# GpSimd's second sum of two pairs made to wait for Vector's two, in the last part of a gated mix of a state-space convolution and a spectral filter

## The chip, the cores and the metric

One core of one Trainium2 chip. The metric is the device time of one execution in microseconds; the median of three runs stands for a kernel. Lower is better. All data are float32.

## The reference

The input u is a sequence of 2048 positions by 640 channels. Two results are made of it and mixed by a gate that depends on the position:

```python
    g = _sigmoid((x * gate_w).sum(-1, keepdims=True))
    a = _A_ref(...)   # y = irfft(rfft(u, 4096) * rfft(K, 4096))[:2048] + u * D_skip, K made of exponentials of the position
    b = _B_ref(...)   # irfft2(rfft2(x) * (w_r + 1j * w_i))
    return g * a + (1 - g) * b
```

Branch a is a long convolution along the sequence, one kernel K per channel, done with transforms of length 4096. Branch b is a filter on the two-dimensional spectrum. Only branch a, in its last part, is touched by the change.

## The kernel before, in words

The transforms are written as matrix products. A transform of length 4096 has two stages: 64 values at a time (`stage1`, L335), then 64 at a time with the twiddle factors folded into the tables (`stage2`, L348). The 640 channels are worked through in four quarters of 160 (index c). A quarter's spectrum is a set of 33 small blocks, two to a column; 17 columns (16 full ones of 128 partitions, and one half, of 64) make a quarter. A column's 128 partitions hold two blocks of 64 (j = 0 and 1).

Earlier parts make the spectrum of u (kept in DRAM as `u_d`), the kernels K (`k_d`), and branch b up to its last stage (`s3e_d`). The last part, `phase_d`, starts at about 438 us of the profile. For each quarter it takes groups of four columns (`groups`; the half column is a group by itself), and for each group:

- `fronts`: per *pair* of columns, `stage2` makes the spectrum of K in PSUM (`p_s`, L348, one of three double banks). Vector multiplies it with the spectrum of u (`us`, loaded from `u_d`) in two products: `ma` (L795: real by real, imaginary by imaginary) and `mb` (L796: crosswise). One input of each lies in PSUM, the other in SBUF. Then come four sums, which make the complex product `t2` out of them: for each block j the difference of the two halves of `ma` (L800, the real part, into partitions 0 to 63 of `t2`), and the sum of the two halves of `mb` (L801, the imaginary part, into partitions 64 to 127). Both inputs of a sum lie in SBUF. Vector takes the real part of j = 0 and the imaginary part of j = 1, and GpSimd the other two, so a full pair costs each engine one L800 and one L801, each 64 partitions by 320 elements.
- `backs`: one or two groups later (the list `late`), the first stage of the inverse transform (L814, `p_i`, reading `t2`), a copy by ScalarE into `s3` (L816, for the half column L818), and the DMA of that to `s3_d` on ScalarE's queue (L823, for the half column L820).

Beside these run, at rates that `merge` sets, `stage1` of the next quarter (L335, with ScalarE's copy L336), and the last stage of branch b and of branch a: `last_e` (TensorE `p_e` at L160, Vector's gated product `oe` at L876) and `last_c` (TensorE `p_c` at L893, Vector's gated product `ot` at L898, and the add of both on GpSimd, L899, with the DMA of the result, L901). The three kinds of `p_s`, and `p_i`, share three PSUM buffers; `p_e` and `p_c` share two. After the last group, `s3_d`'s last rows are written (L820, L823) and read again (L866), and the last products (L893, L896) and output DMAs (L904) end the kernel.

Each engine works its instructions in the order in which they stand in its queue. That order comes from the tile layer, which sorts what the streams issue by when it estimates it to be ready; a semaphore wait is put in wherever an instruction depends on another engine's.

## Time and profile before

| | |
|---|---|
| median of three runs | 607.03 us (604.68 to 610.24) |
| the profiled execution | 608.74 us, span of its instructions 607.0 us |
| granted TensorE clock, mean | 0.966 (1.00 from 438 to 578 us) |
| busy over the span: PE / DVE / ACT / POOL | 535.8 / 500.2 / 364.8 / 267.0 us |
| busy from 438 to 578 us: PE / DVE / ACT / POOL | 128.18 / 118.81 / 40.17 / 73.59 us of 140 |

PE is TensorE (PEld its weight loads), DVE is Vector, ACT is ScalarE, POOL is GpSimd, SP is the engine that only issues DMAs. A line of a group reads: line, engine, operation, out<-in, shape, count | busy us, mean ns of one | idle time of that engine just before, and what ended it. A line of the timeline reads: start and duration in us, engine, line, operation, count, and in brackets how long the engine had been idle and who released it. [...] ACTq and SPq are the queues in which an engine issues DMAs; a piece named DMA in the chain of waits is the transfer itself.

### The profile page before, as it was taken

To read this page: it belongs to the slowest core of one execution; us is meant where nothing else is said; L and a number is where in the kernel's file an instruction comes from. 1 tells how busy PE (TensorE), PEld (TensorE's weight loads), DVE (VectorE), ACT (ScalarE), POOL (GpSimd) and SP (SyncE) were. 2 spreads that over 40 slices of the span, in tenths; PEclk is the share of its full clock that TensorE was granted. 3 is DMA by queue.
4 is the path that set the end of the run, shared out by engine and by line. 5 is a ranking of instruction groups with operands and counts; after the bars stand their busy time and mean duration, and the time that the engine had idled before them with its cause. 6 is when DMAs were issued, how large, how long until landed. Compare 5 with 4: busy or idle time off the path is not lost.

```text
span 607.0 us, 16654 instructions
## 1 busy us (share of the span) xinstructions
PE 535.8 (88%) x7084; PEld 405.6 (67%) x7084; DVE 500.2 (82%) x748; ACT 364.8 (60%) x659; POOL 267.0 (44%) x246
## 2 busy tenths in 40 slices
PE   9688979989968989989798999898989999999874
PEld 7576657766656657676566676565878877787631
DVE  5971597598899989999999899979399796987974
ACT  4556775576846876888589888799723332231210
POOL 4931252053525344454326335416254347547441
PEclk9899989989989996998899999999999999999998
DMA  8787204245612320332250233006685989889776
GB/s 341 293 288 268 79 5 151 69 154 181 239 43 67 97 87 13 108 118 109 67 151 12 75 97 110 24 28 200 224 346 184 356 273 299 291 271 310 225 231 239
DMA packets 48083, 101.98 MB, mean 168 GB/s; under 512 B 3316, under 2 KB 32776, under 8 KB 46248
## 3 DMA queue, kind: packets, MB, share of 16 engines
q1 hardware_dynamic: 24888, 67.74, 32.3%
q10 hardware_dynamic: 20080, 22.52, 11.9%
q0 software_dynamic: 3040, 10.65, 5.3%
q8 instruction: 56, 0.92, 0.6%
q14 instruction: 19, 0.16, 0.1%
HBM read 60.91 MB, written 39.98 MB: 166 GB/s over the span
## 4 chain that ended last, share of the span: by engine, by line
PE 51%; DVE 27%; ACT 9%; DMA 8%; issue 4%; POOL 1%; ACTq 0%; DVEq 0%; POOLq 0%; SPq 0%
PE p_eo L551 8%; PE p_s L348 8%; PE p_s L335 6%; PE p_e L638 5%; PE p_k L693 4%; PE p_i L814 4%; PE p_p L649 3%; DVE q L652 3%; PE p_d L518 2%; DVE t L801 2%; PE p_i L565 2%; PE p_t L502 2%; DVE ma L795 2%; PE p_c L893 2%; PE p_d L519 2%
## 5 line engine op out<-in xcount | busy, mean ns | idle before, releaser
L679 POOL TENSOR_TENSOR y<-e,sc 128x512 f32<-128x512 f32 x40 | 56.7, 1418 | 131.0 <-ACT sc L665 60.3
L348 PE MATMUL p_s<-t,w 128*64 128x160 f32 x1056 | 92.4, 314 | 10.2 <-ACT ut L382 5.1
L348 PEld LDWEIGHTS p_s<-t,w 128*64 128x64 f32 x1056 | 76.5, 139 | 21.4 <-ACT ut L382 6.0
L640 ACT ACTIVATE e<-p_e 128x512 f32<-128x512 f32 x120 | 68.6, 602 | 22.7 <-PE p_e L638 20.4
L551 PE MATMUL p_eo<-td,pmt 107*128 107x321 f32 x204 | 69.0, 459 | 3.9 <-ACT pmt L505 3.9
L693 PE MATMUL p_k<-x,y 128*32 128x64 f32 x2560 | 63.6, 229 | 9.8 <-DVE x L677 2.9
L693 PEld LDWEIGHTS p_k<-x,y 128*32 128x32 f32 x2560 | 46.1, 113 | 38.0 <-issue 29.4
L652 DVE SCALAR_TENSOR_TENSOR q<-q,p_p 128x512 f32<-128x512 f32 x80 | 53.4, 681 | 13.5 <-ACT q L651 11.8
L336 ACT COPY t<-p_s 128x512 f32<-128x512 f32 x40 | 24.6, 623 | 65.2 <-PE p_s L335 41.8
L638 PE MATMUL p_e<-rm,par 128*128 128x512 f32 x120 | 58.7, 519 | 3.4 <-ACT e L640 2.8
L680 POOL TENSOR_TENSOR y<-e,sc 128x512 f32<-128x512 f32 x40 | 54.5, 1362 | 6.5 <-ACT sc L666 6.5
L800 POOL TENSOR_TENSOR t<-ma 64x320 f32<-64x320 f32 x32 | 28.0, 875 | 61.4 <-DVE ma L795 51.8
L551 PEld LDWEIGHTS p_eo<-td,pmt 107*128 107x128 f32 x204 | 38.4, 198 | 19.6 <-ACT pmt L505 6.9
L677 DVE TENSOR_TENSOR x<-e,cx 128x1024 f32<-128x1024 f32 x40 | 48.6, 1214 | 2.2 <-ACT cx L668 2.2
L651 ACT ACTIVATE q<-p_p 128x512 f32<-128x512 f32 x80 | 46.5, 592 | 4.2 <-PE p_p L649 3.8
L649 PE MATMUL p_p<-rp,par 128*128 128x512 f32 x80 | 43.5, 548 | 4.5 <-DVE q L652 4.5
L814 PE MATMUL p_i<-t,w 128*64 128x160 f32 x528 | 42.7, 300 | 4.4 <-POOL t L801 3.4
L335 PE MATMUL p_s<-c,kt 128*64 128x128 f32 x640 | 43.0, 274 | 3.9 <-DVE mb L796 2.0
L335 PEld LDWEIGHTS p_s<-c,kt 128*64 128x64 f32 x640 | 38.0, 136 | 12.6 <-issue 7.7
L816 ACT COPY s<-p_i 128x640 f32<-128x640 f32 x32 | 21.8, 694 | 40.0 <-PE p_i L814 30.4
L335 PE MATMUL p_s<-c,u 128*64 128x128 f32 x640 | 41.5, 278 | 2.5 <-ACT ut L382 2.5
L795 DVE TENSOR_TENSOR ma<-p_s,us 128x640 f32<-128x640 f32 (+1 forms) x36 | 28.2, 784 | 18.8 <-PE p_s L348 11.5
(153 smaller groups left out, 1181.5 us busy)
## 6 DMA issues: line engine op xcount, KB each, us to landing
u_d<-ut SPq DMA_DIRECT2D x32, 320.0 KB, 2.6
us<-u_d ACTq DMA_DIRECT2D x16, 640.0 KB, 6.0
s_d<-s ACTq DMA_DIRECT2D x15, 640.0 KB, 8.3
t<-s_d SPq DMA_DIRECT2D x14, 640.0 KB, 5.9
ww<-in_w_l SPq DMA_DIRECT2D x8, 642.0 KB, 4.0
ue<-u_d SPq DMA_DIRECT2D x8, 640.0 KB, 4.4
k_d<-kt SPq DMA_DIRECT2D x4, 1280.0 KB, 7.6
kt<-k_d SPq DMA_DIRECT2D x8, 640.0 KB, 5.9
```

Source lines behind the costliest of these rows:

```text
L335: nc.tensor.matmul(p[64 * ri:64 * ri + 64, j, :], src(i + j), e1[ri], start=True, stop=True)
L348: ins = nc.tensor.matmul(p[64 * j:64 * j + 64, i, 160 * ri:160 * ri + 160], w2[:, x, 64 * ri:64 * ri + 64], t1[:, x // 2 if x < 32 else K0 ...
L551: P.matmul(p[:, :E], st.pmt[:DC, c, w, j, :], tv[:DC, w, c, :], start=c == 0, stop=c == 2)
L638: P.matmul(p[:, :], pars[t], rm[:, c:c + 512], start=True, stop=True)
L640: st.exp = S.activation(ef[:, c:c + 512], p[:, :], AF.Exp)
L649: P.matmul(p[:, :], pars[t], rp[:, c:c + 512], start=True, stop=True)
L652: V.scalar_tensor_tensor(out=qf[:, c:c + 512], in0=qf[:, c:c + 512], scalar=MAGIC, in1=p[:, :], op0=ALU.subtract, op1=ALU.subtract)
L677: V.tensor_tensor(out=x[:, 0].rearrange("p d (h j) -> p d h j", h=2), in0=e[:, :, 0:64].rearrange("p d (h j) -> p d h j", h=2), in1=cx.uns ...
L679: G.tensor_tensor(out=y[:, 1], in0=e[:, :, 64:96], in1=sc[:, 0], op=ALU.mult)
L680: G.tensor_tensor(out=y[:, 0], in0=e[:, :, 64:96], in1=sc[:, 1], op=ALU.mult)
L693: P.matmul(st.pb[32 * r:32 * r + 32, o, :], y[:, ri, 4 * qq + JR[r], :], x[:, ri, 4 * qq + JR[r], :], start=t % 2 + qq + 1 - ri == 0, stop ...
L814: T.mm = P.matmul(p[x:x + 64, i // 2, 160 * (i % 2):160 * (i % 2) + 160], T.w3[:, k0 + h + i, x:x + 64], t2[:, h + i, :], start=True, stop ...
```

## The change

The four sums of a pair are written by a helper `part(eng, j, im)`, and the last line makes GpSimd's imaginary part (j = 0) depend on Vector's last sum of the same pair: on its L801 for a full pair, on its L800 for a half column. Which engine computes which part stays as it is, and so do the shapes. Since the half column has only j = 0, GpSimd has one sum there, and it waits too.

```diff
@@ -794,11 +795,20 @@
             V.tensor_tensor(out=mb[:nl, :hn], in0=pv, in1=uu[:, :, ::-1, :], op=ALU.mult)
-            for j in range(nj):
+            def part(eng, j, im):
                 l = slice(64 * j, 64 * j + 64)
                 o = slice(nj * h + j, nj * (h + hn), nj)
-                (G if j else V).tensor_tensor(out=t2[0:64, o, :], in0=ma[l, :hn, 0, :], in1=ma[l, :hn, 1, :], op=ALU.subtract)
-                (V if j else G).tensor_tensor(out=t2[64:128, o, :], in0=mb[l, :hn, 0, :], in1=mb[l, :hn, 1, :], op=ALU.add)
+                m = mb if im else ma
+                return eng.tensor_tensor(out=t2[64 * im:64 * im + 64, o, :], in0=m[l, :hn, 0, :], in1=m[l, :hn, 1, :], op=ALU.add if im else ALU.subtract)
+            if nj > 1:
+                part(G, 1, 0)
+            last = part(V, 0, 0)
+            if nj > 1:
+                last = part(V, 1, 1)
+            ins = part(G, 0, 1)
+            tc.add_manual_dep(ins.ins, last.ins.name, SYNC, reason="port")
             yield 0.55 * hn
```

`SYNC` is a dependency of the kind that needs a semaphore. In the changed file all four sums have one line, L802; other lines of the last part are 1 lower before the sums and 10 lower behind them than in the changed file (L899 becomes L909, L820 becomes L830).

The queues of TensorE, Vector and SP hold the same instructions in the same order before and after. Two places differ.

On GpSimd's queue, at the end of the second quarter (`t_6306` is the `t2` of its half column, `ot` the add of both branches), before:

```order
L801 TENSOR_TENSOR t_6208<-mb 64x2x160
L801 TENSOR_TENSOR t_6306<-mb 64x160
L899 TENSOR_TENSOR ot<-ot,oe 128x480 x2
L899 TENSOR_TENSOR ot<-ot,oe 128x320
L901 DMA out<-ot 128x1280
```

and now:

```order
L802 TENSOR_TENSOR t_6208<-mb 64x2x160
L909 TENSOR_TENSOR ot<-ot,oe 128x480
L802 TENSOR_TENSOR t_6306<-mb 64x160
L909 TENSOR_TENSOR ot<-ot,oe 128x480
L909 TENSOR_TENSOR ot<-ot,oe 128x320
L911 DMA out<-ot 128x1280
```

One add has moved ahead of the half column's sum.

On ScalarE's queue, at the very end (`s_7085` is the half column of the last quarter, `s_7091` its last group, copied and written in two halves), before:

```order
L823 DMA s_d<-s_7028 128x8x160
L818 COPY s_7085<-p_i_7086 128x160
L816 COPY s_7091<-p_i_7092 128x640
L820 DMA s_d<-s_7085 64x160
L823 DMA s_d<-s_7091 128x4x160
L816 COPY s_7091<-p_i_7103 128x640
```

and now:

```order
L833 DMA s_d<-s_7028 128x8x160
L828 COPY s_7085<-p_i_7086 128x160
L830 DMA s_d<-s_7085 64x160
L826 COPY s_7091<-p_i_7092 128x640
L833 DMA s_d<-s_7091 128x4x160
L826 COPY s_7091<-p_i_7103 128x640
```

The small DMA of the half column has moved ahead of the copy of the last group's first half. That DMA writes a row that the larger DMA ahead of it (`s_7028`) also writes, and waits until that one has landed.

## The prediction

> **What bounds the kernel now.** I read the windows view first, to see which engine has room in the last part (438 to 578 us, the four quarters of columns; what follows is its tail), then the groups by shape, then the timeline of one pair, and last the waits on TensorE. Columns of the windows rows: stretch, its length, busy us (instructions) of PE, PEld, DVE, ACT and POOL, granted clock, DMA share, GB/s.

> ```profile
> 438.00:457.00 19.00, 16.08 (x216) 13.61 (x216) 17.02 (x22) 4.49 (x8) 9.57 (x11) 1.00 0.83 321
> ...
> 489.00:514.00 25.00, 24.05 (x302) 20.02 (x300) 18.68 (x28) 7.67 (x12) 15.17 (x17) 1.00 0.94 302
> ...
> 560.00:578.00 18.00, 15.00 (x170) 11.47 (x168) 17.37 (x26) 4.46 (x7) 8.10 (x10) 1.00 0.73 230
> ```

> Two engines take turns. From 438 to 457 and from 560 to 578 Vector is busy nearly all the time (17.02 of 19, 17.37 of 18) and TensorE is not. From 489 to 514 it is the reverse: TensorE 24.05 of 25 us. A cheaper Vector is worth something only in stretches of the first kind. The groups say what Vector does there:

> ```profile
> L801 DVE TENSOR_TENSOR t<-mb 64x320 f32<-64x320 f32 x30 | 31.5, 1052 | 0.9
> ...
> L800 DVE TENSOR_TENSOR t<-ma 64x320 f32<-64x320 f32 x30 | 19.1, 638 | 0.0
> ```
> ```profile
> L801 POOL TENSOR_TENSOR t<-mb 64x320 f32<-64x320 f32 x30 | 30.2, 1005 | 2.6 <-DVE mb L796 0.4
> L800 POOL TENSOR_TENSOR t<-ma 64x320 f32<-64x320 f32 x30 | 26.3, 876 | 58.3 <-DVE ma L795 48.7 <-issue 9.6
> ```

> The same shape, 64x320, costs Vector 638 ns as its first sum (L800) and 1052 ns as its second (L801). One pair in order of time (start, duration) shows why:

> ```profile
> 446.20 0.82 DVE L795 TENSOR_TENSOR ma<-p_s,us 128x640 f32<-128x640 f32 x1
> 446.94 0.81 DVE L796 TENSOR_TENSOR mb<-p_s,us 128x640 f32<-128x640 f32 x1
> 447.67 0.63 DVE L800 TENSOR_TENSOR t<-ma 64x320 f32<-64x320 f32 x1
> 448.34 1.04 DVE L801 TENSOR_TENSOR t<-mb 64x320 f32<-64x320 f32 x1
> 449.41 0.82 DVE L795 TENSOR_TENSOR ma<-p_s,us 128x640 f32<-128x640 f32 x1
> ```
> ```profile
> 447.10 0.86 POOL L800 TENSOR_TENSOR t<-ma 64x320 f32<-64x320 f32 x1 [1.28 <-DVE ma L795]
> 448.04 0.99 POOL L801 TENSOR_TENSOR t<-mb 64x320 f32<-64x320 f32 x1
> ```

> GpSimd's first sum ends at 447.10 + 0.86 = 447.96, and Vector's first at 448.30, 0.34 us later. GpSimd's second ends at 449.03, and Vector's second at 449.38, 0.35 us later. Whatever its start, Vector's sum ends a fixed third of a microsecond behind GpSimd's: it stands until GpSimd is through. Where GpSimd happened to be late, the first sum is short:

> ```profile
> 457.17 0.81 DVE L796 TENSOR_TENSOR mb<-p_s,us 128x640 f32<-128x640 f32 x1
> 457.90 0.47 DVE L800 TENSOR_TENSOR t<-ma 64x320 f32<-64x320 f32 x1
> 458.41 1.05 DVE L801 TENSOR_TENSOR t<-mb 64x320 f32<-64x320 f32 x1
> ```
> ```profile
> 456.77 0.86 POOL L800 TENSOR_TENSOR t<-ma 64x320 f32<-64x320 f32 x1 [1.29 <-DVE ma L795]
> 458.07 1.04 POOL L801 TENSOR_TENSOR t<-mb 64x320 f32<-64x320 f32 x1 [0.43 <-DVE mb L796]
> ```

> Here GpSimd's first sum was over (457.63) before Vector's began, and that took 0.47 us. The second, behind GpSimd's end at 459.11, again ends 0.35 us later (459.46). The products are not touched: mb takes 0.81 us beside GpSimd's sum (446.94), and ma 0.82 where GpSimd stands (446.20 and 449.41).

> [...]

> **The change part by part.** No instruction is added or removed. In each pair GpSimd's second sum now waits for Vector's second.

> *Vector's second sum.* It is never seen alone. Bounds: 0.35 us (what it takes behind GpSimd's end) and 1.05 (if its length is its own). I take 0.47, from the first sum at 457.90, the same shape alone. Saved: 1.04 - 0.47 = 0.57 us.

> *Vector's first sum.* It still meets GpSimd's first, so it keeps ending 0.34 us behind that. But GpSimd now comes later. Count from the end of Vector's second sum: GpSimd's second sum starts at 0.08 (GpSimd's first starts 0.08 after ma's end, 447.02 to 447.10), takes 0.87 (its first sum beside mb took 0.86; the bound above is the 1.04 of a blocked one) and ends at 0.95. Its next first sum starts at 1.03 (the gap from 447.96 to 448.04) and ends at 1.89. Vector's first sum ends at 2.23, its second starts 0.04 later and ends at 2.74. So the pair falls from 3.21 us (446.20 to 449.41) to 2.74: **0.47 saved**, with the loop now through both engines. Where a gated product stands between two pairs, GpSimd has time, its first sum is not late, and the full 0.56 or so is saved.

> *What that is worth on the path.* Only TensorE's gaps can be given back. Those in this part that Vector ends are here, with one that ScalarE ends, at 472.81, for later (start, duration, gap and releaser in brackets; the last row is of the weight loads):

> ```profile
> 447.90 1.09 PE L335 MATMUL p_s<-c,kt 128*64 128x128 f32 x16 [1.96 <-DVE mb L796]
> ...
> 457.31 0.76 PE L160 MATMUL p_e<-t3e,c 128*64 128x320 f32 x4 [0.93 <-DVE oe L876]
> ...
> 472.81 1.37 PE L348 MATMUL p_s<-t,w 128*64 128x160 f32 x16 [0.69 <-ACT t L336]
> ...
> 486.30 1.36 PE L348 MATMUL p_s<-t,w 128*64 128x160 f32 x16 [0.52 <-DVE mb L796]
> 488.54 1.03 PE L160 MATMUL p_e<-t3e,c 128*64 128x480 f32 x4 [0.88 <-DVE oe L876]
> ...
> 505.19 0.76 PE L893 MATMUL p_c<-t,c 128*64 128x320 f32 x4 [0.50 <-DVE ot L898]
> ```
> ```profile
> 526.00 1.34 PE L348 MATMUL p_s<-t,w 128*64 128x160 f32 x16 [0.47 <-DVE mb L796]
> 528.24 1.03 PE L160 MATMUL p_e<-t3e,c 128*64 128x480 f32 x4 [0.89 <-DVE oe L876]
> ...
> 544.39 1.41 PE L814 MATMUL p_i<-t,w 128*64 128x160 f32 x17 [0.39 <-DVE mb L796]
> ...
> 562.25 1.31 PE L814 MATMUL p_i<-t,w 128*64 128x160 f32 x16 [0.62 <-DVE mb L796]
> 564.49 0.76 PE L160 MATMUL p_e<-t3e,c 128*64 128x320 f32 x4 [0.93 <-DVE oe L876]
> 568.29 1.03 PE L160 MATMUL p_e<-t3e,c 128*64 128x480 f32 x4 [0.81 <-DVE oe L876]
> 572.49 0.20 PEld L160 LDWEIGHTS p_e<-t3e,c 128*64 128x64 f32 x4 [0.44 <-DVE oe L876]
> ```

> By stretch, a gap shrinks by what Vector has saved by then in that stretch, and no further than to nothing. Around 447.90 two pairs are done: 0.94 of the 1.96 goes. At 457.31 five are done (2.35): the whole 0.93. Then 486.30 and 488.54 come after three and four pairs: 0.52 + 0.88 = 1.40 whole. 505.19: 0.50. 526.00 and 528.24: 1.36. 544.39: 0.39. In the last quarter the first pair saves nothing, since GpSimd, late there from an earlier add, made Vector's first sum short already and will block the second as before:

> ```profile
> 555.72 0.47 DVE L800 TENSOR_TENSOR t<-ma 64x320 f32<-64x320 f32 x1
> ```
> ```profile
> 555.82 1.12 POOL L800 TENSOR_TENSOR t<-ma 64x320 f32<-64x320 f32 x1
> ```

> So at 572.49 four pairs have saved 2 x 0.47 + 2 x 0.56 = 2.06 of the 2.80 us of gaps. Sum: 0.94 + 0.93 + 1.40 + 0.50 + 1.36 + 0.39 + 2.06 = **7.6 us**.

> *What is late now.* t2 is complete some 0.5 us later after a pair's start (2.70 + 0.08 + 0.87 = 3.65 us, against 449.38 - 446.20 = 3.18). Its readers, the products p_i, run one or two groups behind and don't notice, except at the end:

> ```profile
> 585.11 1.39 PE L814 MATMUL p_i<-t,w 128*64 128x160 f32 x16 [1.82 <-POOL t L801]
> ```

> There TensorE waits for that very sum (the last pair's), and would be through at 587.0 instead of 586.5, but its result is not next on the path, as the tail shows. The add moved ahead of a half-size sum on GpSimd's queue costs nothing: that sum's reader comes a group later.

> *The tail.* On ScalarE's queue the small DMA L820 now stands ahead of the copy L816. Before, that copy ran at 583.34, while L820 was still waiting for the large DMA to land:

> ```profile
> 577.86 8.84 DMA s_d<-s
> ...
> 586.79 0.48 ACTq L820
> ...
> 587.37 0.54 ACTq L823
> ...
> 587.96 0.70 ACT s L816
> ```
> ```profile
> 583.34 0.69 ACT L816 COPY s<-p_i 128x640 f32<-128x640 f32 x1 [2.67 <-PE p_i L814]
> ```

> Now it runs after L820, and its DMA and the last copy behind it: 0.69 us put on the path, with small change **0.65 lost** (bounds: nothing, if the large DMA lands before the products are through; 1.24, copy and DMA together). The last copy then starts near 588.6 on the old clock, and the late p_i, over by 587.0, hides under it.

> Net: 7.6 - 0.65 = 6.9 us. The profiled execution took 608.74, so 601.8 by its own time; the median of the three timed runs is 607.03, and the same gain from there gives **600.1 us**, which I forecast.

> **The rivals.** *TensorE keeps most of it.* With Vector ahead, the next wait is the turn from one quarter to the next, where ScalarE's copy ends the gap (0.69 at 472.81), or a slot that ScalarE frees. For: TensorE is at 24.05 of 25 in the middle stretch. Against: the gaps above name Vector. If half of the 7.6 is lost so, 3.8 - 0.65 = 3.2 us are left: 603.9.

> *The length is the second sum's own*, say because of its upper 64 partitions. For: no row shows it short. Against: the 0.34 and 0.35 us behind GpSimd's end. Then a pair grows by the 0.09 that GpSimd's first sum is late, some 20 pairs on the path by 1.8, with the tail 2.4: 609.5.

> *The product is blocked instead: slower.* ma now runs beside GpSimd's second sum. If that held it off until GpSimd's end, ma would take up to 0.87 more each time, against 0.47 saved: 0.40 x 20 pairs (five, four, four and five in Vector's stretches, two at the end) = 8, with the tail 8.7: 615.7. It decides from 0.82 + 0.47 = 1.29 us for one ma. Against it: mb beside GpSimd's other sum takes 0.81.

> **How the numbers follow.** Forecast 0.72 (4 to 11 us gained; above 6.9 if smaller stalls of TensorE's weight loads, which I left out, go too), TensorE keeps it 0.16, the sum's own length 0.06, product blocked 0.06. The range: above, to 605.0, which takes in the second case; below, to 594.5: all 9.3 us of the gaps shown gone, the tail free, and the runs' own spread (2 to 3 us either side of their median) on top. Within 1% (6 us, about what a measurement here can tell from no change) means over 601.0: the sum ends just beyond it, so a quarter of the forecast's chance falls short. Faster by over 1%: 0.64; within 1%: 0.29; slower: 0.07.

> **What the profile would show.** Right: Vector's L801 sums (L802 there) at 0.47 us, not 1.05; GpSimd's second sum beside ma, at 0.87; ma still 0.82; a pair back to back in 2.74; TensorE's gaps at the gated products gone; the copy ahead of the last DMA now behind L820. Wrong: Vector's second sum still near 1.05; ma over 1.2; or Vector idle before ma, with TensorE's gaps now ended by ScalarE or GpSimd.

## The result and the profile after

The changed kernel took 600.28 us (median of 6 runs, 595.31 to 603.87), the kernel before 607.85 us (6 runs, 604.68 to 610.24, on the same chip). The ratio is 0.9881, with a 95% interval of 0.9844 to 0.9918: 7.6 us, or 1.2%, are gained. The forecast was 600.1 us. Executions over 1.5% above the fastest of their kernel count as slow, and the ratios with their intervals, here and below, leave them out, while the medians are of all executions. The profiled execution of the changed kernel took 599.81 us (span 598.0 us, clock 0.965).

What Vector and GpSimd do in the last part comes first: the groups by shape of the changed kernel, from 426 us to the end. L802 is the line of all four sums.

```profile
L796 DVE TENSOR_TENSOR ma<-p_s,us 128x640 f32<-128x640 f32 x32 | 26.3, 822 | 24.4 <-PE p_s L349 14.8 <-issue 7.8 <-POOL t L802 1.4
...
L802 DVE TENSOR_TENSOR t<-ma 64x320 f32<-64x320 f32 x32 | 21.4, 669 | 0.0
L802 DVE TENSOR_TENSOR t<-mb 64x320 f32<-64x320 f32 x32 | 16.2, 507 | 1.0
```
```profile
L802 POOL TENSOR_TENSOR t<-ma 64x320 f32<-64x320 f32 x32 | 28.0, 876 | 34.1 <-DVE ma L796 23.6 <-issue 9.5
L802 POOL TENSOR_TENSOR t<-mb 64x320 f32<-64x320 f32 x32 | 27.7, 865 | 30.0 <-DVE t L802 30.0
```

Vector's second sum (from `mb`) takes 507 ns, where it took 1052. The products stay at 822 ns. The first sum has grown from 638 to 669 ns. GpSimd's second sum is a little shorter too (865 ns, from 1005) and is released by Vector's. One pair in order of time, first on Vector and then on GpSimd, shows how they now stand to each other:

```profile
449.21 0.83 DVE L796 TENSOR_TENSOR ma<-p_s,us 128x640 f32<-128x640 f32 x1
449.96 0.81 DVE L797 TENSOR_TENSOR mb<-p_s,us 128x640 f32<-128x640 f32 x1
450.69 0.74 DVE L802 TENSOR_TENSOR t<-ma 64x320 f32<-64x320 f32 x1
451.46 0.49 DVE L802 TENSOR_TENSOR t<-mb 64x320 f32<-64x320 f32 x1
451.98 0.82 DVE L796 TENSOR_TENSOR ma<-p_s,us 128x640 f32<-128x640 f32 x1
```
```profile
449.26 0.88 POOL L802 TENSOR_TENSOR t<-mb 64x320 f32<-64x320 f32 x1 [0.94 <-DVE t L802]
450.22 0.87 POOL L802 TENSOR_TENSOR t<-ma 64x320 f32<-64x320 f32 x1
```

GpSimd's second sum of the pair before (449.26 to 450.14) lies beside `ma` and the start of `mb`. Its first sum of this pair begins only when that is over and ends at 451.09. Vector's first sum ends at 451.43, again 0.34 us behind it; Vector's second then runs alone, in 0.49. (Neighbours on Vector overlap by up to 0.08 us in these rows: the first `ma` ends at 450.04, and `mb` starts at 449.96.) In both profiles 94 of Vector's sums began while one of GpSimd's ran, and 93 of them ended 0.34 to 0.35 us behind the end of GpSimd's (the other, of a half column, 0.18). From one `ma` to the next it is 2.77 us, where it was 3.21.

TensorE's gaps in the same stretches (start, duration, and in brackets the idle time and who ended it), the last one from the tail:

```profile
448.18 1.09 PE L336 MATMUL p_s<-c,kt 128*64 128x128 f32 x16 [1.22 <-DVE mb L797]
454.19 1.83 PE L161 MATMUL p_e<-t3e,c 128*64 128x480 f32 x8 [1.59 <-DMA t3e<-s3e_d]
...
524.70 1.03 PE L161 MATMUL p_e<-t3e,c 128*64 128x480 f32 x4 [0.23 <-DVE oe L886]
...
559.14 0.76 PE L161 MATMUL p_e<-t3e,c 128*64 128x320 f32 x4 [0.45 <-DVE oe L886]
...
575.68 1.75 PE L824 MATMUL p_i<-t,w 128*64 128x160 f32 x16 [2.13 <-POOL t L802]
```

Of the gaps that Vector ended before (0.4 to 2.0 us each) 0.2 to 0.5 is left, and 1.22 of the first one's 1.96. There is a new one, at 454.19: TensorE waits 1.59 us for a DMA. And the wait for GpSimd's last sums has grown from 1.57 to 2.13 us at its first occurrence (575.68).

To see in which quarter the time was gained, I measure everything from the first `ma` of the part. Below are its rows on Vector at four points, the first `ma` of the first, second and last quarter and that of the last group, before and after:

```profile
439.67 0.83 DVE L795 TENSOR_TENSOR ma<-p_s,us 128x640 f32<-128x640 f32 x1 [8.81 <-PE p_s L348]
...
474.27 0.83 DVE L795 TENSOR_TENSOR ma<-p_s,us 128x640 f32<-128x640 f32 x1 [4.72 <-issue]
...
554.25 0.82 DVE L795 TENSOR_TENSOR ma<-p_s,us 128x640 f32<-128x640 f32 x1 [1.35 <-PE p_s L348]
...
579.02 0.82 DVE L795 TENSOR_TENSOR ma<-p_s,us 128x640 f32<-128x640 f32 x1 [1.37 <-POOL t L801]
```
```profile
440.98 0.82 DVE L796 TENSOR_TENSOR ma<-p_s,us 128x640 f32<-128x640 f32 x1 [8.80 <-PE p_s L349]
...
474.40 0.82 DVE L796 TENSOR_TENSOR ma<-p_s,us 128x640 f32<-128x640 f32 x1 [4.88 <-issue]
...
549.86 0.82 DVE L796 TENSOR_TENSOR ma<-p_s,us 128x640 f32<-128x640 f32 x1 [1.35 <-PE p_s L349]
...
572.06 0.82 DVE L796 TENSOR_TENSOR ma<-p_s,us 128x640 f32<-128x640 f32 x1 [1.44 <-POOL t L802]
```

The first quarter took 474.27 - 439.67 = 34.60 us before and takes 33.42 now; the second and third together 79.98 and 75.46; the last, up to its last group, 24.77 and 22.20. That makes 139.35 and 131.08: 8.27 us are gained in the body of the part. This measure is far sharper than a median: three kernels without the wait (before, and two below) agree in it to 0.11 us, while whole executions of one kernel differ by 5 us and more.

### The profile page after: what moved, and what is told of

Read it like the earlier page. It is cut to its first block, busy times and chain, and to the rows that moved or that the text cites. A ratio compares the mean times of both kernels' runs of the same rounds, so it can differ in the third digit from the quotient of the medians.

```text
span 598.0 us, 16655 instructions
## 1 busy us (share of the span) xinstructions
PE 532.4 (89%) x7084; PEld 407.2 (68%) x7084; DVE 483.7 (81%) x748; ACT 364.8 (61%) x659; POOL 262.7 (44%) x246
## 5 line engine op out<-in xcount | busy, mean ns | idle before, releaser
L349 PE MATMUL p_s<-t,w 128*64 128x160 f32 x1056 | 90.7, 309 | 10.3 <-ACT ut L383 7.0
L694 PE MATMUL p_k<-x,y 128*32 128x64 f32 x2560 | 61.1, 223 | 10.3 <-DVE x L678 3.1
L694 PEld LDWEIGHTS p_k<-x,y 128*32 128x32 f32 x2560 | 44.0, 109 | 37.9 <-issue 28.8
L796 DVE TENSOR_TENSOR ma<-p_s,us 128x640 f32<-128x640 f32 (+1 forms) x36 | 28.2, 784 | 25.5 <-PE p_s L349 14.8
L824 PE MATMUL p_i<-t,w 128*64 128x160 f32 x528 | 44.7, 307 | 3.3 <-POOL t L802 3.1
L336 PE MATMUL p_s<-c,kt 128*64 128x128 f32 x640 | 43.4, 274 | 3.8 <-DMA kt<-k_d 2.1
L336 PEld LDWEIGHTS p_s<-c,kt 128*64 128x64 f32 x640 | 38.6, 136 | 12.0 <-issue 5.9
L336 PE MATMUL p_s<-c,u 128*64 128x128 f32 x640 | 43.0, 285 | 2.6 <-ACT ut L383 2.6
L826 ACT COPY s<-p_i 128x640 f32<-128x640 f32 x32 | 21.7, 694 | 38.7 <-PE p_i L824 23.3
L802 POOL TENSOR_TENSOR t<-mb 64x320 f32<-64x320 f32 (+1 forms) x36 | 29.8, 827 | 34.0 <-DVE t L802 33.9
```

Of the source, the lines that this page charges most:

```text
L336: nc.tensor.matmul(p[64 * ri:64 * ri + 64, j, :], src(i + j), e1[ri], start=True, stop=True)
L349: ins = nc.tensor.matmul(p[64 * j:64 * j + 64, i, 160 * ri:160 * ri + 160], w2[:, x, 64 * ri:64 * ri + 64], t1[:, x // 2 if x < 32 else K0 ...
L694: P.matmul(st.pb[32 * r:32 * r + 32, o, :], y[:, ri, 4 * qq + JR[r], :], x[:, ri, 4 * qq + JR[r], :], start=t % 2 + qq + 1 - ri == 0, stop ...
L824: T.mm = P.matmul(p[x:x + 64, i // 2, 160 * (i % 2):160 * (i % 2) + 160], T.w3[:, k0 + h + i, x:x + 64], t2[:, h + i, :], start=True, stop ...
```

## The experiments

All kernels are told by their edit to the changed kernel. The table has the median of the timed runs, the ratio to the kernel before on the same chip, and from the profiled execution the three lengths just defined, with one more: from the last group's first `ma` to the start of ScalarE's last copy (L826, before L816), and from there to the end of Vector's last operation.

| kernel | median us | ratio (95%) | 1st quarter | 2nd + 3rd | last, to its last group | to last copy | to the end |
|---|---|---|---|---|---|---|---|
| before | 607.85 | 1 | 34.60 | 79.98 | 24.77 | 8.94 | 15.59 |
| changed | 600.28 | 0.9881 (0.9844-0.9918) | 33.42 | 75.46 | 22.20 | 8.81 | 13.74 |
| changed, again | 599.53 | 0.9882 (0.9844-0.9921) | 33.41 | 75.34 | 22.17 | 8.80 | 15.60 |
| no wait | 608.2 | 0.9987 (0.9955-1.0018) | 34.61 | 79.97 | 24.75 | 7.52 | 13.92 |
| both sums wait | 602.12 | 0.9891 (0.9843-0.9939) | 34.60 | 74.61 | 21.83 | 8.61 | 14.70 |
| last group free | 600.48 | 0.9887 (0.9841-0.9932) | 33.86 | 75.33 | 22.17 | 9.42 | 15.37 |
| first three quarters | 601.25 | 0.9878 (0.9829-0.9926) | 35.72 | 75.34 | 24.75 | 8.53 | 14.07 |
| last quarter only | 606.04 | 0.9932 (0.9892-0.9972) | 34.58 | 79.94 | 22.18 | | |
| early load | 600.12 | 0.9803 (0.9723-0.9882) | 32.01 | 75.31 | 22.17 | 8.80 | 13.86 |
| early load, again | 599.22 | 0.9856 (0.9805-0.9906) | 32.01 | 75.31 | 22.15 | 8.46 | 13.81 |
| early load, no wait | 606.93 | 0.9953 (0.9906-1.0001) | 34.59 | 79.91 | 24.74 | 7.52 | 16.08 |
| early load, last group free | 598.78 | 0.9851 (0.9804-0.9898) | 32.01 | 75.31 | 22.15 | 9.59 | 15.40 |
| early load, both sums wait | 597.85 | 0.9879 (0.9819-0.9939) | 31.83 | 74.67 | 21.87 | 9.13 | 14.94 |

(The tail of "last quarter only" is left out, since its profiled execution, 610.57 us, was far above the median of the kernel.)

**No wait.** The code as rewritten, with the one line of the dependency left out. All queues then stand as before the change.

```diff
-            tc.add_manual_dep(ins.ins, last.ins.name, SYNC, reason="port")
```

> The four sums are written in the changed order, but nothing waits. Every queue stands as in the kernel before, so the theory (the wait alone, by letting Vector's second sum run free of GpSimd's, gives the gain) expects the time of before: 607.9, within 2 us, with Vector's second sum at 1.05 us again. A rival, that the order of writing moved something, expects some of the 7.6 us: below 604.

It took 608.2 us against 608.49 before, and its body is that of before in every quarter. Vector's second sum (groups on Vector):

```profile
L802 DVE TENSOR_TENSOR t<-mb 64x320 f32<-64x320 f32 x32 | 33.6, 1050 | 1.0
```

1050 ns with GpSimd beside it, 507 with GpSimd held back, from one semaphore: the length was not the second sum's own. That ends the second rival.

**Both sums wait.** GpSimd's first sum waits for Vector's two as well. Its queue then has the sum from `mb` ahead of the one from `ma`.

```diff
-            if nj > 1:
-                part(G, 1, 0)
             last = part(V, 0, 0)
...
             tc.add_manual_dep(ins.ins, last.ins.name, SYNC, reason="port")
+            if nj > 1:
+                tc.add_manual_dep(part(G, 1, 0).ins, last.ins.name, SYNC, reason="port")
```

> Both of GpSimd's sums of a pair wait for Vector's second. By the theory (Vector's sum stands until GpSimd's is through, a product does not) a pair that follows a pair directly stays at about 2.75 us: GpSimd is through at 1.90 after Vector's second sum and Vector's first ends at 2.24. Where a gated product stands between, Vector's first sum falls from 0.65 to 0.47. The end: t2 is 0.9 us later per pair, which only the last group can feel. Time: 598 to 602, as the changed kernel. The rival, that the products are slowed too when GpSimd has two sums beside them, expects ma or mb above 0.9 us and a time above 604.

A piece of Vector's timeline of this kernel, the first two pairs of the part, shows what it does to the first sum:

```profile
443.22 0.47 DVE L802 TENSOR_TENSOR t<-ma 64x320 f32<-64x320 f32 x1
443.73 0.49 DVE L802 TENSOR_TENSOR t<-mb 64x320 f32<-64x320 f32 x1
444.25 0.82 DVE L796 TENSOR_TENSOR ma<-p_s,us 128x640 f32<-128x640 f32 x1
...
445.72 0.79 DVE L802 TENSOR_TENSOR t<-ma 64x320 f32<-64x320 f32 x1
...
447.06 0.82 DVE L796 TENSOR_TENSOR ma<-p_s,us 128x640 f32<-128x640 f32 x1
```

The first pair of a run, with GpSimd idle, has both sums short (0.47 and 0.49). In the next, GpSimd still works on the first pair's two sums when Vector comes to its own: 0.79. Two sums of 0.87 us take GpSimd longer than the two products last (1.47 us here, 444.25 to 445.72), so back to back the pair is again about 2.8 us (444.25 to 447.06), whichever of them waits. Where TensorE sets the pace and pairs stand apart, both sums are short (over all pairs the means are 578 and 489 ns, 669 and 507 in the changed kernel); quarters two to four gain 0.85 + 0.37 us more than in the changed kernel. Where the changed kernel's first quarter took 33.42 us, all of that gain was lost again: 34.60 us, with the same wait for a DMA, here at its longest:

```profile
456.16 1.83 PE L161 MATMUL p_e<-t3e,c 128*64 128x480 f32 x8 [2.98 <-DMA t3e<-s3e_d]
```

**Last group free.** The wait is left out for the last group of the last quarter; ScalarE's queue then has the order of before (the copy L826 ahead of the small DMA L830).

```diff
-            tc.add_manual_dep(ins.ins, last.ins.name, SYNC, reason="port")
+            if (c, g0) != (3, 12):
+                tc.add_manual_dep(ins.ins, last.ins.name, SYNC, reason="port")
```

> The wait is left out in the last group alone (two pairs); ScalarE's queue then stands as before, with the copy ahead of the small DMA. By the prediction's tail term (0.65 us lost by the moved copy) this kernel is 0.6 us faster than the changed one; and TensorE, which in the changed kernel waited 2.1 us for GpSimd in the last group and then ran at half clock, would wait 1.6 and keep the clock at 1.00, so that the last copy starts 1 to 2 us sooner: 598 to 599. The rival, that the early landing of the large DMA in the changed kernel (5.5 us against 8.8) came from that move, expects this kernel to be slower than the changed one by some 2 us: 602.

600.48 us: no difference from the changed kernel that can be measured, and the last copy comes no sooner (9.42 us behind the last group's first `ma`, against 8.81), where 1 to 2 us sooner had been expected. In its profile the small DMA L831 got away only 7.70 us after the issue of the large one (575.32 to 583.02), and the last copy followed 1.16 us behind it. What else the two tails differ in is read below.

**First three quarters, and last quarter only.** The wait in a part of the quarters. ScalarE's order at the end is that of before in the first of these, and that of the change in the second.

```diff
-            tc.add_manual_dep(ins.ins, last.ins.name, SYNC, reason="port")
+            if c < 3:
+                tc.add_manual_dep(ins.ins, last.ins.name, SYNC, reason="port")
```

The second kernel has `if c == 3:` in that place.

> The wait only in the first three quarters. By the sum of gaps these hold 0.94 + 0.93 + 1.40 + 0.50 + 1.36 + 0.39 = 5.5 of the 7.6 us (5.7 in the two profiles, from the first pair to the last quarter's first), and the last quarter runs as before: 602.4, if the tail is as before. The rival, that the gain came in the last quarter and the tail (in the profiles the end moved 10.3 us against the first pair, 4.6 of it in the last quarter and behind it), expects 5.7 at most from here too, but the whole from a kernel that waits in the last quarter alone; here it is the time between the first pair and the last quarter's first that decides: 114.5 as before, or 108.8 as changed.

> The wait only in the last quarter. By the sum of gaps that quarter holds 2.06 of the 7.6 us (2.5 in the two profiles), with the tail of the changed kernel: 606 by the theory, and the first three quarters to the hundredth as before (114.6 us from the first pair to the last quarter's first). The rival, that the last quarter and the tail gave more than the gaps (4.6 us in the profiles), expects 603 to 604.

In the body the gain is a sum by quarter: with the wait in three quarters the last one is as before (24.75), with the wait in the last alone the others are as before (34.58, 79.94) and the last is as changed (22.18). One number is out of line: the first quarter of the first kernel took 35.72 us, more than without any wait. The DMA wait is there too, and what follows it is slow (TensorE, then the windows view: stretch, length, busy us and instructions of PE, PEld, DVE, ACT, POOL, then granted clock, DMA share, GB/s):

```profile
453.03 3.36 PE L161 MATMUL p_e<-t3e,c 128*64 128x480 f32 x8 [2.21 <-DMA t3e<-s3e_d]
```
```profile
453.00:456.00 3.00, 2.97 (x8) 0.93 (x10) 1.86 (x3) 0.00 (x0) 1.70 (x2) 0.53 0.08 27
```

After 2.21 us without work TensorE got the clock 0.53, and the eight matmuls `p_e` took 3.36 us where the row of the changed kernel has 1.83.

**Early load.** What TensorE waits for there is the first load of `t3e` (1280 KB, L864), whose issue stands on SP's queue behind three loads of tables (`w`, 704 KB each). It waits 1.58 to 2.98 us in every kernel that has the sums' wait in this quarter and the load in this place. The edit puts the load ahead of the tables.

```diff
     def load_e(c):
-        nc.sync.dma_start(t3es[c][:, :, :], ...)
+        T.le = nc.sync.dma_start(t3es[c][:, :, :], ...)
...
-                    with behind(T.ki[1, 0]):
+                    with behind(T.ki[1, 0]), behind(T.le):
                         nc.sync.dma_start(T.w3[:, k:k + 11, :], ...)
```

> The changed kernel, with the first load of branch b's rows (t3e) put ahead of the three large table loads (w3) on SP's queue. In every kernel with the wait seen so far TensorE stood 1.6 to 3.0 us for that load in the first quarter, so that of the 1.87 us expected there only 1.2 came in the changed kernel, and 0.0 and -1.1 in two others. By the theory (Vector's freed time was there, a DMA ended the wait) the first quarter now falls from 34.60 us to below 33.0, and the time to 598.5 to 599.5. The rival, that TensorE's own work or ScalarE ends the first quarter, expects 33.4 again and 600.3.

SP's queue in the changed kernel and in this one:

```profile
433.15 1.53 SPq L947 DMA_DIRECT2D w<-in_t_w  x3
...
442.21 1.12 SPq L864 DMA_DIRECT2D t3e<-s3e_d  x1
```
```profile
441.35 0.32 SPq L864 DMA_DIRECT2D t3e<-s3e_d  x1
441.72 4.14 SPq L947 DMA_DIRECT2D w<-in_t_w  x3
```

Counted from the first `ma` (440.98 and 441.68), the load is issued 1.56 us sooner: 0.33 ahead of it, not 1.23 behind. The tables, 7.83 us ahead of the first `ma` before this edit, now come 0.04 behind it. With the tables behind it and not ahead of it, it also lands quicker, 10.4 us from its issue against 11.9 in the list of DMA issues. TensorE's wait for it is gone. The only gap before `p_e` that is left in this quarter is Vector's:

```profile
456.86 0.76 PE L161 MATMUL p_e<-t3e,c 128*64 128x320 f32 x4 [0.17 <-DVE oe L886]
```

The first quarter takes 32.01 us, and in the repeat the same: 1.41 us less than in the changed kernel. The median, 600.12 us of four executions, does not show it; 598.5 to 599.5 had been expected.

**Early load, no wait.** The same without the dependency.

> The early load alone, without the wait (the sums in the changed order of writing, which leaves the queues as before). In the kernel before, TensorE waited for that load by 0.2 us or less, and Vector's products ended its gaps; so by the theory nothing comes of it: the first quarter at 34.4 to 34.6 us, time 608, within 1.5. The rival, that the load itself is worth something, expects the first quarter below 34.

34.59 us for the first quarter: by itself the early load gains nothing there. The transfer became late only because Vector had become quicker. Its ratio, 0.9953, touches 1 at the edge of its interval.

**Early load, last group free.** Both edits.

> The early load, and the wait everywhere but in the last group, where it costs 0.5 us per pair of t2's lateness and where TensorE's longer idle time came with half its clock. By the theory the fastest version: first quarter below 33.0, clock 1.00 until the last group's products are through, 598. If the last group's wait and the moved DMA don't matter beyond the scatter of the landing of the large DMA (5.5 to 8.9 us so far), it is as the early load with the wait everywhere: 599.

The body is that of the early load (129.47 us), the tail that of the free last group: 598.78 us. That the clock would stay at 1.00 until the last products are through did not come true: they took 2.18 us, not 1.39.

**Repeats.** The changed kernel and the early load once more, on one chip.

> The changed kernel once more, on the same chip and in the same rounds as the next, so that the two can be set side by side: 600 to 601, the first quarter anywhere from 33.4 to 35.7 us, as the landing of the t3e load falls.

> The changed kernel with the early load once more. By the theory the first quarter is 32.0 us again to the hundredth, since no DMA ends a wait in it, and the median lies 1.4 to 3 us below the changed kernel's. The rival, that what is gained in the first quarter is lost again in the tail, expects the same median.

599.53 and 599.22 us. The body repeats itself: 130.92 (131.08 the first time) and 129.47 (129.49). The medians, expected 1.4 to 3 us apart, do not separate the two: whole executions of one kernel scatter by more than the bodies differ.

**Early load, both sums wait.** The two edits that shortened the body, together.

> Both edits that helped apart, in one kernel: both of GpSimd's sums of a pair wait for Vector's two (as where both waited), and the t3e load stands ahead of the three table loads (as in the early load). If the sums' wait and the early load are independent: no wait of p_e for t3e in the first quarter, which then takes no more than the 32.01 us of the early load, quarters two and three 74.6 us and the last 21.8 to its last group, as where both sums waited: 128.4 us from the first ma to the last group's first, against 131.08 in the changed kernel and 139.35 before. The median would then be near 598.5 with the tail as it scatters (within 2 us). Rival: where both sums waited, the body was shorter only because TensorE had been held up by 3 us in the first quarter and made that up later; then with the early load the body is that of the early load alone, 129.5, and the median 599 to 600.

The lengths add up as if the edits knew nothing of each other: 31.83, 74.67 and 21.87, a body of 128.37 us, 10.98 less than before and 2.71 less than in the changed kernel. The median, 597.85 us, is the lowest of all; its interval (0.9819 to 0.9939) overlaps with those of the others, so as a time of the kernel it is not shown to be better than the changed one.

## Why the prediction was right, and where its sizes were not

The mechanism came out step by step; the three stretches and the tail had other sizes, which in part offset one another in the median.

**The sums and the pair.** Forecast 0.47 for Vector's second sum, 0.34 behind GpSimd's end for the first, 2.74 for the pair; measured 0.49 (0.507 in the mean, with the exception below), 0.34 and 2.77. The product was not blocked (0.82 beside GpSimd's sum throughout; its rival decided from 1.29). The sums, with both inputs in SBUF, took 1050 ns beside GpSimd's and 507 with GpSimd held back. The products, with one input in PSUM, took 0.81 to 0.83 us in the changed kernel, the 52 that a sum of GpSimd's ran beside and the 12 that none did. Why the sums are held up and the products are not, no run tests. The exception that was forecast is there as well: in the last quarter's first pair GpSimd is late and blocks the second sum as before. Vector, then GpSimd, in the changed kernel:

```profile
551.84 1.05 DVE L802 TENSOR_TENSOR t<-mb 64x320 f32<-64x320 f32 x1
```
```profile
551.42 1.11 POOL L802 TENSOR_TENSOR t<-ma 64x320 f32<-64x320 f32 x1
```

**The first quarter: 1.87 forecast, 1.18 measured, 2.59 without a wait that I missed.** The step that failed is that a gap of TensorE shrinks by what Vector saves: the load of `t3e` had been done just in time before (issued at 441.03 and 11.5 us under way, so landed at 452.5, where TensorE's weight load waited 0.2 us for it), and I asked of every transfer whether the change delays it, not whether it is now wanted sooner. The early load shows both sides: 2.59 us gained with it, nothing without the sums' wait. The row of the load in the list of DMA issues, before:

```profile
t3e<-s3e_d SPq DMA_DIRECT2D x1, 1280.0 KB, 11.5
```

That 2.59 is more than 1.87 has the reason that the next two quarters show as well: with the early load TensorE's busy time in this quarter fell too, from 30.94 to 29.94 us for the same 418 matmuls.

**The second and third quarters: 3.65 forecast, 4.52 measured.** The sum was of idle time alone. Over the two quarters, before and after (windows view: stretch, length, then busy us and instructions of PE and the other engines):

```profile
474.27:554.25 79.98, 75.08 (x947) 61.60 (x944) 66.40 (x94) 23.33 (x38) 44.95 (x49) 1.00 0.91 298
474.40:549.86 75.46, 73.98 (x947) 61.92 (x944) 57.85 (x94) 23.36 (x38) 42.82 (x49) 1.00 0.92 316
```

TensorE's idle time fell from 4.90 to 1.48 us, by 3.42, close to the sum. The other 1.10 us came out of its busy time, for the same 947 matmuls. That these were stalls too short to stand as gaps in the list, such as the prediction named and left out, is my estimate: before which matmuls they stood I have not worked out. TensorE, then, did not keep the gain; the first rival had its sign wrong in these quarters.

**The last quarter: 2.06 forecast, 2.57 measured.** I counted up to the last gap in the list and so left out the pair behind it; five pairs save, not four, which by the same 0.47 and 0.56 us makes 2.6.

**The tail: 0.65 lost by forecast.** The queue did change as forecast, but what it costs depends on when the large DMA lands. ScalarE in the tail of the changed kernel, and in the repeat of the early load:

```profile
577.98 0.49 ACTq L830 DMA_DIRECT2D s_d<-s  x1
578.57 0.69 ACT L826 COPY s<-p_i 128x640 f32<-128x640 f32 x1 [4.68 <-DMA s_d<-s]
579.29 0.36 ACTq L833 DMA_DIRECT2D s_d<-s  x1
580.87 0.69 ACT L826 COPY s<-p_i 128x640 f32<-128x640 f32 x1 [1.61 <-PE p_i L824]
```
```profile
575.66 0.48 ACTq L830 DMA_DIRECT2D s_d<-s  x1
576.24 0.69 ACT L826 COPY s<-p_i 128x640 f32<-128x640 f32 x1 [5.68 <-DMA s_d<-s]
576.96 0.36 ACTq L833 DMA_DIRECT2D s_d<-s  x1
577.36 0.69 ACT L826 COPY s<-p_i 128x640 f32<-128x640 f32 x1 [0.43 <-PE p_i L824]
```

In the changed kernel the large DMA (of `s_7028`) let L830 go 5.5 us after its own issue, and not 8.9 as in the profile before. ScalarE was through with the moved copy and then stood 1.61 us for TensorE's last products: the copy cost nothing, as the lower bound had it. In the repeat of the early load the same DMA took 7.2 us, and the last copy follows as fast as the queue lets it (its row names TensorE, but those products were through at 576.98, while the queue issued L833 until 577.32): 577.36 - 575.66 = 1.70 us behind L830, where in the old order it was 1.17 (587.96 - 586.79 in the prediction's rows). So the term is 0.53 us where the landing decides, and nothing where it does not.

What the tail lost instead is at its products. With an early landing and the old order the last copy began 7.52 us behind the last group's first `ma` (no wait, and early load, no wait); in the changed order 8.80 (changed, again, and early load). Of these 1.28 us, 0.27 is the later start of the last products (578.42 - 572.06 = 6.36 us, against 585.11 - 579.02 = 6.09): GpSimd's late sum, which I had found harmless. The other 1.01 is their length, 2.40 us instead of 1.39, since the clock was halved (windows view of the changed kernel):

```profile
576.00:578.00 2.00, 1.43 (x16) 0.90 (x12) 1.41 (x3) 0.00 (x0) 1.05 (x2) 0.60 1.29 466
578.00:580.00 2.00, 1.58 (x12) 1.43 (x14) 0.00 (x0) 0.69 (x1) 0.37 (x1) 0.50 0.16 51
```

The wait ahead of it was 2.13 us, and 1.57 without the change. With the last group free the two waits were 1.26 and 1.82 us, and the clock stayed at 1.00 (that the longer wait alone halves the clock is not shown, as the last section tells):

```profile
577.64 1.39 PE L825 MATMUL p_i<-t,w 128*64 128x160 f32 x16 [1.26 <-POOL t L802]
580.86 1.39 PE L825 MATMUL p_i<-t,w 128*64 128x160 f32 x16 [1.82 <-POOL t L802]
```

**How it came to the right median.** Measured against 7.6 - 0.65 us: a body of 8.27, and a tail that changed by -0.13 us up to the last copy in the two profiled executions (8.94 to 8.81), because the early landing in the second paid for the slow products. Between the first `ma` and the last copy 8.4 us were gained, where 6.9 had been forecast. That the time, 600.28 us, met the forecast to 0.2 is therefore luck in part: the body gave more and the tail took less than forecast, the scatter behind the last copy hides it in the medians, and the forecast started from a median of three runs, 607.03, where six gave 607.85. From the last copy to the end it is anything from 13.7 to 16.1 us, whatever the kernel; this stretch holds the last write of `s_d` and its reading back. Up to 2.3 us of the difference between executions lies there, and no experiment here explains it, nor why the large DMA lands in 5.5 us at one time and 8.9 at another. The order on ScalarE's queue may have a hand in it: in the changed order the small DMA got away 5.5 to 5.7 us after the large one's issue in five of six profiles and 7.2 in the sixth; in the order of before 6.8 to 8.9 in five of six, and 5.6 in the other. Nothing here tests that.

## What to carry to other kernels

When an engine is made faster, list the loads that its part waits for and ask which arrived with little to spare: one of them was the next wait here, and took 1.41 of 2.59 us. Look for one shape with two durations on an engine (here 507 and 1050 ns for Vector's sum, 865 and 1005 for GpSimd's): it showed two engines holding each other up. What helped was to put one engine's operation beside one of the other's that was not held up (a product, 0.82 us with and without a sum of GpSimd's beside it), counting what then comes late at the end of the loop. To judge an edit of one microsecond in a kernel whose runs differ by five, measure between two fixed instructions of the trace: that put the early load 1.5 us ahead of the changed kernel and repeated to 0.2 us, where the medians of the two could not be told apart.

## What the runs showed of the hardware

TensorE's clock fell after shorter pauses than I had reckoned with. In the tail it was halved behind a wait of 2.1 to 2.3 us in each of the six kernels that kept the wait everywhere, so the change's half microsecond there seemed to be the cause. But of the other six ("last quarter only" is left out), with waits of 1.3 to 1.6 and 1.8 us, two were halved too (first three quarters; early load, last group free). The first of them, with the same second wait as in the kernel with the last group free, which kept its clock:

```profile
581.11 2.40 PE L825 MATMUL p_i<-t,w 128*64 128x160 f32 x16 [1.82 <-POOL t L802]
```

Here the clock fell at 579.48, only 0.2 us into that wait; the wait before it was 1.56 us. In the first quarter 2.21 us sufficed in one kernel (clock 0.53), while 2.98 us did not in another, the one where both sums wait.

```profile
449.77:453.18 3.41, 1.21 (x17) 0.95 (x15) 3.32 (x6) 0.44 (x1) 1.91 (x3) 1.00 0.83 282
```
```profile
454.39:457.80 3.41, 1.64 (x8) 0.63 (x10) 2.17 (x4) 0.00 (x0) 1.73 (x3) 1.00 0.39 150
```

The pause of 2.21 us lay within the first of these steps; TensorE was busy for 1.21 us of it, and at its end the clock was halved. The pause of 2.98 us was cut by the grid point at 454.39, so that 2.19 us of work were left in the step before and 1.64 in the step behind, and the clock stayed. In the last part of the thirteen traces, from 436 us on, a step at full clock with less than 1.4 us of busy TensorE was followed by the half clock each time (14 steps), one with more than 1.7 us never; of the 12 between, three were. (In earlier parts, with other matmuls, a step with 2.08 us in the kernel before and one with 2.09 us in the changed one were still followed by it.) In the tail of the six kernels without the wait in the last group, the emptiest step at full clock had 1.59 to 1.66 us, on the border; with the wait it had 0.76 to 1.53. The longer wait thus leaves less work in a step, and six of six were halved against two of six, but no experiment shifted the grid, so that the wait alone is the cause is not shown.

The clock was halved behind steps with up to 1.66 us of work in this part. The price was 1.0 us for the sixteen matmuls in the tail (2.40 against 1.39) and 1.5 us for eight in the first quarter (3.36 against 1.83).
